# One-core decode kernel: group rows gathered on VectorE, shared weight loads for w2 and wo, w4 in seven pieces

## The chip, the cores and the metric

The kernel runs on one core of one Trainium2 chip. The metric is the device time of one execution in microseconds (us); a few executions are taken for each kernel, in rounds beside the kernel before on the same chip. The profile of one of them gives the trace (the trace of before is of a further execution, outside the timed ones). The *span* that a profile prints runs from the first to the last instruction and is about 1.8 us shorter than the time of the same execution (403.8 and 405.56). All executions here count as undisturbed ("fast") by the usual test.

Engines: PE is the matrix engine, PEld its weight loads, DVE is VectorE, ACT is ScalarE, POOL is GpSimd, SP issues the loads.

## The reference, cut to what matters

Two blocks read the same normalised row and are added. Block A is attention for one token: 32 query heads, 4 key/value heads, 65,536 keys. Block B is a small mixer with two linear layers w1 and w2 and an MLP w3, w4.

```python
x = A_x; xn = _layernorm(x)
out = x + A(xn, k_cache, v_cache, wq, wo) + B(xn, w1, w2, w3, w4)
# A: q = xn @ wq; softmax(q k^T / sqrt(128)) v, then @ wo       (4096 x 1024)
# B: h = gelu(layernorm(xn) @ w1), each quarter of h shifted along the sequence;
#    with a sequence of one, every shifted quarter is zero
#    x1 = xn + hs @ w2;  out = x1 + gelu(layernorm(x1) @ w3) @ w4   (w4: 3584 x 1024)
```

Everything is bf16. The caches are 67 MB each and the weights 36 MB, so 169.87 MB have to be read, once. As the shifted h is zero, w2 multiplies zeros and w1's result is not used; both kernels compute them all the same.

## The kernel before: the parts that matter

All inputs stream through three buffers of 8 MB in a fixed order: wq, w3, w1 and w2 together, then K and V of eight units (K7, wo, V7 at the end), then w4. When a buffer is released, the next load is issued. The result is summed in one bank, `psB`: the left half of the output row in partition 0, the right half in partition 32.

```python
W4_PIECES = (16, 8, 2, 1, 1)        # chunks of 256 KB, one DMA each

def row_acc(j, lhsT, rhs):           # one row of output, half j, on its own column tile
    nc.tensor.matmul(psB[32 * j:32 * j + 1, :], lhsT=lhsT, rhs=rhs, start=False, stop=False,
                     tile_position=(0, 32 * j), skip_group_check=True)

def group_rows(g, og, lp):           # gather the eight heads of a group out of 128 x 512
    for cg in range(4):              # fp32 matmuls against a 0/1 matrix
        nc.tensor.matmul(pe[:, 0:P], lhsT=selbig[:, cg, :], rhs=og[:, 128 * cg:128 * (cg + 1)], ...)
    nc.tensor.matmul(pe[:, P:P + 1], lhsT=sel8big[:], rhs=lp[:, 0:1], ...)
    ...                              # mask, reduce, divide -> oT[g], 128 x 8 bf16

def project(g):                      # oT[g] times its part of wo
    for j in range(8):
        for h2 in range(2):
            row_acc(h2, oT[g][:, j:j + 1], wt[:, g, j, 512 * h2:512 * (h2 + 1)])

compute_k(NU - 1)
for g in range(HKV - 1):
    project(g)                       # groups 0 to 2, while V7 is on its way
compute_v(NU - 1)                    # V7, then group_rows(3)
project(HKV - 1)
compute_w4(0, FC)                    # 28 chunks x 2 matmuls into psB
# copy psB to SBUF, store 2 KB
```

A pass over the finished program drops a weight load when the same weights already stand at the same tile position.

## Time and profile before

The first three timed executions took 404.04 to 404.27 us, median 404.18. The profiled one took 405.56 us.

| what | value | where |
|---|---|---|
| bytes read | 169.87 MB at 421 GB/s | page, queues |
| 16 DMA engines busy with the inputs | 97.6% of the span | page, queues |
| PE busy, DVE busy | 59%, 49% | page, engines |
| wait of PE before the last 24 matmuls | 2.22 us | timeline |

From the profile page of the kernel before, the head, the DMA part and one line of the groups (line of the source, engine, operation, output and inputs, count, then busy us and mean ns, then idle time before and who ended it):

```profile
span 403.8 us, 2690 instructions
...
q1 hardware_dynamic: 4128, 169.87, 97.6%
q8 instruction: 9, 0.15, 0.1%
...
L180 PE MATMUL psB<-big,hT 128*1 128x512 bf16 x56 | 8.1, 452 | 2.2 <-DMA big<-in_B_w_dram 2.2
```

The input queue is nearly always busy. "q8 instruction" is nine packets of 16 KB with which an engine's program itself is fetched.

The PE part of the timeline of the kernel before, from V7 to the end (start us, us, engine, line, operation, then idle time before and who ended it):

```profile
386.08 1.16 PE L398 MATMUL pm_e<-og,selbig 128*128 128x128 f32 x8 [0.86 <-DVE og L389]
387.07 0.28 PE L399 MATMUL pm_e<-lp,sel8big 128*128 128x1 f32 x2
388.41 1.89 PE L180 MATMUL psB<-big,oT 128*1 128x512 bf16 x16 [1.06 <-DVE oT L409]
390.14 3.62 PE L180 MATMUL psB<-big,hT 128*1 128x512 bf16 x32
395.98 4.44 PE L180 MATMUL psB<-big,hT 128*1 128x512 bf16 x24 [2.22 <-DMA big<-in_B_w_dram]
```

Read from below: the last 24 matmuls of w4 take 185 ns each, where the 32 before them took 113 ns. The windows view of the same trace shows why (stretch, its length, busy us and counts of PE, PEld, DVE, ACT and POOL, then the granted clock of PE, the mean share of the DMA engines that is busy, GB/s):

```profile
393.19:396.61 3.42, 1.20 (x12) 0.40 (x10) 0.00 (x0) 0.00 (x0) 0.00 (x0) 1.00 0.69 271
396.60:400.00 3.40, 3.40 (x18) 1.08 (x16) 0.00 (x0) 0.00 (x0) 0.00 (x0) 0.50 0.03 12
```

After a stretch of 3.42 us with the 2.22 us wait in it, the clock is halved for the next 3.41 us. The Trainium skill says in "TensorE: Matmul & The Clock Gate", Part 1, that PE's clock is set by a free-running window of about 3.4 us and halves after an idle one; the clock steps of this trace are indeed multiples of 3.413 us.

One more reading is needed, and the printed views give it only in part: when each load has landed. A load is done when the slowest of the 16 DMA engines is ("DMA: Bandwidth & Descriptors", section "Why a DMA increments its semaphore by 16 and not by 1", says that they finish independently). The trace agrees: for the last chunk of w4 the first engine is done at 395.12 us and the last at 398.42.

### The profile page before, as it was taken

What the parts mean: (1) busy time and instruction counts of PE and PEld (TensorE: products, weight loads), DVE (VectorE), ACT (ScalarE), POOL (GpSimd) and SP (SyncE); (2) the same over time, 40 slices, a digit from 0 to 9 for tenths busy, and PEclk for the clock granted to TensorE, in tenths of its full rate; (3) what the DMA queues carried; (4) which work ended last, traced back from release to release, by engine and by line L of the source; (5) the groups of instructions that cost most, each with busy time, mean ns of one, the idle gap of its engine ahead of it and who ended that gap; (6) DMA issues with size and microseconds to landing.
All of it is one profiled execution on the core that took longest, in us unless ns stands there. A gap on an engine that the chain in (4) does not pass through costs nothing.

```text
span 403.8 us, 2690 instructions
## 1 busy us (share of the span) xinstructions
PE 236.7 (59%) x1392; PEld 51.5 (13%) x952; DVE 197.1 (49%) x141; ACT 27.0 (7%) x35; POOL 5.5 (1%) x29
## 2 busy tenths in 40 slices
PE   5161972691678349742955394649265923787384
PEld 2010110010200120010102110201030101002131
DVE  4000000965296459525943793288439651964010
ACT  1000020003000200020001002000200020002000
POOL 2000000000000000000000000000000000000000
PEclk9995776597679686958896698659776978798698
DMA  9999999999999999999999999999999999999992
GB/s 403 428 392 410 446 454 467 422 416 416 424 461 461 416 411 422 428 474 430 416 422 435 443 441 435 416 428 443 448 435 422 411 435 407 430 476 428 403 409 80
DMA packets 4144, 170.03 MB, mean 421 GB/s; under 512 B 419, under 2 KB 421, under 8 KB 806
## 3 DMA queue, kind: packets, MB, share of 16 engines
q1 hardware_dynamic: 4128, 169.87, 97.6%
q8 instruction: 9, 0.15, 0.1%
q14 instruction: 1, 0.01, 0.0%
q10 hardware_dynamic: 6, 0.00, 0.0%
HBM read 169.87 MB, written 0.00 MB: 421 GB/s over the span
## 4 chain that ended last, share of the span: by engine, by line
DMA 51%; DVE 18%; PE 14%; ACT 2%; issue 0%; SPq 0%; DVEq 0%; ACTq 0%
DMA big<-in_A_k_cache_dram 43%; DVE big L325 14%; DMA big<-in_B_w_dram 8%; PE sc L330 7%; PE oacc L380 4%; PE psB L180 2%; DVE p_sb L351 2%; DVE mx L335 2%; ACT p_sb L348 2%; PE ps L301 1%; PE pm_mx L337 0%; DVE m L339 0%; PE pm_mx L344 0%; DVE rep L341 0%; ACT out_t L438 0%
## 5 line engine op out<-in xcount | busy, mean ns | idle before, releaser
L330 PE MATMUL sc<-big,qdiag 128*128 128x512 bf16 x512 | 129.9, 415 | 62.6 <-DVE big L325 62.4
L325 DVE STREAM_TRANSPOSE big<-big 128x4096 f32<-128x4096 f32 x32 | 139.4, 4413 | 50.6 <-DMA big<-in_A_k_cache_dram 50.6
L380 PE MATMUL oacc<-big,p_sb 128*32 128x512 bf16 x512 | 46.2, 540 | 41.9 <-DVE p_sb L351 34.5
L330 PEld LDWEIGHTS <-qdiag 128*128 128x128 bf16 x128 | 13.2, 103 | 173.0 <-issue 140.7
L335 DVE TENSOR_REDUCE mx<-sc 128x1 f32<-128x2048 f32 x8 | 18.3, 2292 | 29.9 <-PE sc L330 29.9
L348 ACT ACTIVATE p_sb<-sc,nball 128x2048 bf16<-128x2048 f32 x8 | 15.7, 1967 | 219.0 <-DVE nball L346 219.0
L351 DVE STREAM_TRANSPOSE p_sb<-p_sb 128x2048 bf16<-128x2048 bf16 x8 | 18.5, 2311 | 18.0 <-ACT p_sb L348 18.0
L380 PEld LDWEIGHTS <-p_sb 128*32 128x32 bf16 x512 | 17.2, 130 | 68.1 <-DVE p_sb L351 35.1
L247 PE MATMUL psh<-big,ln_rep_b 128*32 128x512 bf16 x56 | 14.2, 1049 | 8.6 <-DMA big<-in_B_w_dram 8.6
L389 DVE SCALAR_TENSOR_TENSOR og<-oacc,wb,og 128x512 f32<-128x512 f32 x4 | 3.0, 750 | 30.7 <-PE oacc L380 30.7
L337 PE MATMUL pm_mx<-ident_f,mx 128*1 128x128 f32 x8 | 2.4, 296 | 19.1 <-DVE mx L335 19.1
L247 PE MATMUL psq<-big,ln_rep_a 128*32 128x512 bf16 x64 | 6.2, 571 | 11.2 <-DMA big<-in_A_wq_dram 11.2
L293 DVE CAST hT<-pm_h 128x24 bf16<-128x24 f32 x1 | 0.3, 264 | 25.1 <-PE pm_h L291 25.1
L180 PE MATMUL psB<-big,oT 128*1 128x512 bf16 x64 | 8.9, 443 | 1.1 <-DVE oT L409 1.1
L259 DVE CAST q_row<-psq 128x512 bf16<-128x512 f32 x1 | 0.7, 691 | 18.1 <-PE psq L247 18.1
L180 PE MATMUL psB<-big,hT 128*1 128x512 bf16 x56 | 8.1, 452 | 2.2 <-DMA big<-in_B_w_dram 2.2
L274 POOL COPY qdiag<-qx 32x32 bf16<-32x32 bf16 x16 | 3.2, 203 | 280.0 <-PE sc L330 250.5
L398 PE MATMUL pm_e<-og,selbig 128*128 128x128 f32 x32 | 4.6, 288 | 3.5 <-DVE og L389 3.5
L344 PE MATMUL pm_mx<-ident_f,rep 1*128 1x1 f32 x8 | 1.8, 228 | 5.0 <-DVE rep L341 5.0
L386 ACT COPY og<-oacc 128x512 f32<-128x512 f32 x4 | 2.3, 586 | 33.7 <-PE oacc L380 33.7
L398 PEld LDWEIGHTS pm_e<-og,selbig 128*128 128x128 f32 x32 | 3.9, 191 | 5.4 <-DVE og L389 5.4
L337 PEld LDWEIGHTS pm_mx<-ident_f,mx 128*1 128x1 f32 x8 | 0.6, 79 | 28.2 <-DVE mx L335 28.2
(96 smaller groups left out, 65.2 us busy)
## 6 DMA issues: line engine op xcount, KB each, us to landing
big<-in_A_wo_dram SPq DMA_DIRECT2D x1, 8192.0 KB, 37.2
big<-in_B_w_dram SPq DMA_DIRECT2D x1, 7168.0 KB, 38.5
big<-in_B_w_dram SPq DMA_DIRECT2D x3, 2048.0 KB, 40.8
big<-in_B_w_dram SPq DMA_DIRECT2D x1, 4096.0 KB, 27.4
big<-in_B_w_dram SPq DMA_DIRECT2D x1, 512.0 KB
big<-in_B_w_dram SPq DMA_DIRECT2D x2, 256.0 KB, 33.3
big<-in_A_k_cache_dram SPq DMA_DIRECT2D x8, 41.7
big<-in_A_v_cache_dram SPq DMA_DIRECT2D x8, 36.8
```

The lines of the kernel that those rows point to most:

```text
L180: nc.tensor.matmul(psB[32 * j:32 * j + 1, :], lhsT=lhsT, rhs=rhs, start=False, stop=False, tile_position=(0, 32 * j), skip_group_check=True)
L247: nc.tensor.matmul(acc[32 * q:32 * q + 32, i, :], lhsT=rep[:, c, :], rhs=cols(c, 2 * q + i), start=(c == 0), stop=(c == DC - 1), tile_posi ...
L274: nc.gpsimd.tensor_copy(out=qdiag[at, LEAD:].rearrange("p (x c) -> p x c", x=4)[:, :, 32 * a:32 * a + 8], in_=qx[at, :, 8 * g:8 * g + 8])
L301: nc.tensor.matmul(ps1[32 * q:32 * q + 32, 0, :], lhsT=xn2_rep[:, c, :], rhs=wt[:, 0, c, 512 * q:512 * (q + 1)], start=(c == 0), stop=(c = ...
L325: nc.vector.transpose(out=words, in_=words)
L330: nc.tensor.matmul(sc[:, e, :], lhsT=qdiag[:, c0:c0 + P], rhs=cols[:, s, e, :, b2, :, r], start=(s == 0 and b2 == 0 and r == 0), stop=(s = ...
L335: nc.vector.reduce_max(out=mx[:], in_=sc[:].rearrange("p e n -> p (e n)"), axis=AX.X)
L337: nc.tensor.transpose(pm[0:1, 0:P], mx[:, 0:1], ident_f[:])
L348: nc.scalar.activation(out=p_sb[:], in_=sc[:], func=ACTF.Exp, bias=nball[:, b:b + 1], scale=SCALE, accum_out=group["lall"][:, b:b + 1])
L351: nc.vector.transpose(out=flat, in_=flat)
L380: nc.tensor.matmul(oacc[32 * q:32 * (q + 1), :], lhsT=pT[:, e, 32 * t:32 * (t + 1)], rhs=vt[:, :, e, t, :], start=(e == 0 and t < 4), stop ...
L398: nc.tensor.matmul(pe[:, 0:P], lhsT=selbig[:, cg, :], rhs=og[:, 128 * cg:128 * (cg + 1)], start=(cg == 0), stop=(cg == 3))
```

## The change

The intent: take the fp32 gather matmuls and many weight loads off PE, and let w4 arrive in pieces that shrink, so that little work is left when the last piece lands. The diff, cut to its core:

```diff
-W4_PIECES = (16, 8, 2, 1, 1)
+W4_PIECES = (11, 6, 4, 3, 2, 1, 1)
...                                   # w1: both halves on one column tile, w2: one zero column for all
-                row_acc(j, gT[:, c:c + 1], wt[:, 1, c, 512 * j:512 * (j + 1)])
+                row_acc(j, g_col[:], wt[:, 1, c, 512 * j:512 * (j + 1)])
...                                   # group_rows
-        for cg in range(4):
-            nc.tensor.matmul(pe[:, 0:P], lhsT=selbig[:, cg, :], rhs=og[:, 128 * cg:128 * (cg + 1)], ...)
-        nc.tensor.matmul(pe[:, P:P + 1], lhsT=sel8big[:], rhs=lp[:, 0:1], start=True, stop=True)
+        nc.vector.tensor_tensor(out=own, in0=own, in1=mask4[:]..., op=ALU.mult)
+        nc.vector.tensor_reduce(out=ol[:, 0:DH], in_=og[:].rearrange("p (s d) -> p d s", d=DH), ...)
+        nc.tensor.matmul(pe[:, 0:DH + 1], lhsT=sel8big[:], rhs=ol[:], start=True, stop=True)
...                                   # project: one column tile, two banks of its own
-                row_acc(h2, oT[g][:, j:j + 1], wt[:, g, j, 512 * h2:512 * (h2 + 1)])
+                nc.tensor.matmul(tail["rows"][0:1, h2, :], lhsT=oT[g][:, j:j + 1], rhs=..., tile_position=(0, 0))
+    def add_projection():
+        rows = ppool.tile([1, 2, 512], F32, name="o_rows", tag="p")
+        nc.vector.tensor_copy(out=rows[:], in_=tail["rows"][0:1, 0:2, :])
+        for j in range(2):
+            row_acc(j, ident_f[0:1, 0:1], rows[0:1, j, :])
...
+    tail["rows"] = ps_S.tile([P, SUBS, 512], F32, name="o_acc", tag="sc")
...
-    compute_w4(0, FC)
+    compute_w4(0, W4_PIECES[0])
+    add_projection()
+    compute_w4(W4_PIECES[0], FC)
```

The two halves of the row now share one weight load in `project`, but they also share one column tile, so they can no longer run side by side (16 matmuls took 1.89 us on two column tiles in before), and their sum has to be added to `psB` at the end.

More of the change, by code (lines that the diff above doesn't have):

```diff
@@ L173, with row_acc @@
     nc.gpsimd.memset(qdiag[:], 0.0)
-    gT = const.tile([P, DC], BF16, name="gT")
-    nc.gpsimd.memset(gT[:], 0.0)
+    g_col = const.tile([P, 1], BF16, name="g_col")
+    nc.gpsimd.memset(g_col[:], 0.0)
     psB = ps_B.tile([P, 512], F32, name="psB")
-    def row_acc(j, lhsT, rhs):
-        nc.tensor.matmul(psB[32 * j:32 * j + 1, :], lhsT=lhsT, rhs=rhs, start=False, stop=False,
+    def row_acc(j, lhsT, rhs, start=False):
+        nc.tensor.matmul(psB[32 * j:32 * j + lhsT.shape[1], :], lhsT=lhsT, rhs=rhs, start=start, stop=False,
                          tile_position=(0, 32 * j), skip_group_check=True)
@@ L223 @@
     nc.vector.tensor_tensor(out=mask16[:], in0=sel32[:, 0:16], in1=sel32[:, 16:32], op=ALU.add)
-    selbig = const.tile([P, 4, P], F32, name="selbig")
-    nc.vector.tensor_copy(out=selbig[:].rearrange("p c (h d) -> p (c h) d", d=16),
-                          in_=sel32[:].unsqueeze(2).to_broadcast([P, 32, 16]))
+    mask4 = const.tile([P, 4], F32, name="mask4")
+    nc.vector.tensor_reduce(out=mask4[:], in_=sel32[:].rearrange("p (s h) -> p s h", h=8), axis=AX.X, op=ALU.add)
     sel8big = const.tile([P, P], F32, name="sel8big")
@@ L239 @@
     for j in range(2):
-        nc.tensor.matmul(psB[32 * j:32 * j + 32, :], lhsT=ident_f[0:1, 0:32], rhs=accx[0:1, 512 * j:512 * (j + 1)],
-                         start=True, stop=False, tile_position=(0, 32 * j), skip_group_check=True)
+        row_acc(j, ident_f[0:1, 0:32], accx[0:1, 512 * j:512 * (j + 1)], start=True)
     def row_matmul(acc, rep, cols, n_slices):
@@ L300, in compute_w12 @@
             for q in range(2):
-                nc.tensor.matmul(ps1[32 * q:32 * q + 32, 0, :], lhsT=xn2_rep[:, c, :],
-                                 rhs=wt[:, 0, c, 512 * q:512 * (q + 1)], start=(c == 0), stop=(c == DC - 1),
-                                 tile_position=(0, 32 * q), skip_group_check=True)
-        h1 = ppool.tile([64, 512], BF16, name="h1", tag="p")
-        nc.scalar.activation(out=h1[:], in_=ps1[0:64, 0, :], func=ACTF.Gelu_apprx_tanh)
+                nc.tensor.matmul(ps1[0:32, q, :], lhsT=xn2_rep[:, c, :], rhs=wt[:, 0, c, 512 * q:512 * (q + 1)],
+                                 start=(c == 0), stop=(c == DC - 1), tile_position=(0, 0))
+        h1 = ppool.tile([32, 2, 512], BF16, name="h1", tag="p")
+        nc.scalar.activation(out=h1[:], in_=ps1[0:32, 0:2, :], func=ACTF.Gelu_apprx_tanh)
         for c in range(DC):
             for j in range(2):
-                row_acc(j, gT[:, c:c + 1], wt[:, 1, c, 512 * j:512 * (j + 1)])
+                row_acc(j, g_col[:], wt[:, 1, c, 512 * j:512 * (j + 1)])
         st.done("w12")
@@ L362, in group_weights @@
         lw = small.tile([P, NB], F32, name="lw")
-        lp = small.tile([P, 1], F32, name="lp")
+        ol = small.tile([P, DH + 1], F32, name="ol")
         nc.vector.tensor_tensor_reduce(out=lw[:], in0=group["lall"][:], in1=wb[:], scale=1.0, scalar=0.0,
-                                       op0=ALU.mult, op1=ALU.add, accum_out=lp[:])
-        return og, wb, lp
+                                       op0=ALU.mult, op1=ALU.add, accum_out=ol[:, DH:DH + 1])
+        return og, wb, ol
     assert NB == 2
@@ L372, in compute_v @@
         if b == 1:
-            og, wb, lp = group_weights()
+            og, wb, ol = group_weights()
         vt = st.tiles[("V", u)][:].rearrange("p (s u t d) -> p s u t d", u=SUBS, s=SETS, t=16)
@@ L390, in compute_v, with group_rows @@
                                        op0=ALU.mult, op1=ALU.add)
-        group_rows(g, og, lp)
+        group_rows(g, og, ol)
     oT = {}
-    def group_rows(g, og, lp):
+    tail = {}
+    def group_rows(g, og, ol):
         pe = ps_M.tile([P, 512], F32, name="pm_e", tag="pm")
-        for cg in range(4):
-            nc.tensor.matmul(pe[:, 0:P], lhsT=selbig[:, cg, :], rhs=og[:, 128 * cg:128 * (cg + 1)], start=(cg == 0), stop=(cg == 3))
-        nc.tensor.matmul(pe[:, P:P + 1], lhsT=sel8big[:], rhs=lp[:, 0:1],
-                         start=True, stop=True)
+        own = og[:].rearrange("p (s d) -> p s d", d=DH)
+        nc.vector.tensor_tensor(out=own, in0=own, in1=mask4[:].unsqueeze(2).to_broadcast([P, 4, DH]), op=ALU.mult)
+        nc.vector.tensor_reduce(out=ol[:, 0:DH], in_=og[:].rearrange("p (s d) -> p d s", d=DH), axis=AX.X, op=ALU.add)
+        nc.tensor.matmul(pe[:, 0:DH + 1], lhsT=sel8big[:], rhs=ol[:], start=True, stop=True)
         msk = small.tile([P, 16, 8], F32, name="msk", tag="msk")
@@ L414, in project @@
             for h2 in range(2):
-                row_acc(h2, oT[g][:, j:j + 1], wt[:, g, j, 512 * h2:512 * (h2 + 1)])
+                nc.tensor.matmul(tail["rows"][0:1, h2, :], lhsT=oT[g][:, j:j + 1],
+                                 rhs=wt[:, g, j, 512 * h2:512 * (h2 + 1)], start=(g == 0 and j == 0),
+                                 stop=(g == HKV - 1 and j == 7), tile_position=(0, 0))
+    def add_projection():
[3 more added lines that the diff above has]
+            row_acc(j, ident_f[0:1, 0:1], rows[0:1, j, :])
     def compute_w4(lo, hi):
```

## The prediction

> **What bounds the kernel now.** The input stream. The page gives 169.87 MB on one queue, with the 16 DMA engines 97.6% busy with it over the 403.8 us span, 421 GB/s; the row of slices is full until the last slice. DMA issues (timeline of SP) come long before they are needed: the next K or V load is issued about 20 us before the previous one has landed, so nothing that PE or DVE does between 40 and 362 us sets the time. Only the tail does. There (timeline, windows of 0.25 us, landings): V7 lands at 380.2, its matmuls end at 385.2, oT is ready at 388.4, projection of group 3 takes 1.9 us, the 16-chunk piece of w4 3.6 us, PE then waits 2.2 us for the 8-chunk piece (395.98), and its last 24 matmuls take 4.4 us, because the granted clock falls from 1.0 to 0.5 at 396.6 after that wait (213 ns a matmul against 113 ns before). The last bytes land at 398.4; matmuls end at 400.4, copy and store end the span at 403.8. So at most about 1.5 us stand between the last landing and the end of PE's work, and that is all the change can win, apart from a small piece of DMA time.
>
> **What the change does, costed.**
> - Body: fp32 gather matmuls of group_rows (8 records, 1.16 us) become two DVE passes of 128x512 fp32 (about 0.7 us each, estimated from the 128x128 and 128x2048 DVE records) and one 129-column matmul. w1 and w2 get fewer loads but w1 loses its two concurrent column tiles. All off the critical path: 0 us.
> - Projection of groups 0 to 2: it now needs the score banks, so it starts after the exp (368.2, not 365.8), and both halves share one column tile, so they no longer overlap: about 216 ns a matmul warm instead of 113. 48 matmuls, the first ten cold, end near 380.5, just as V7 lands. PE is then warm for V7, whose matmuls started cold before (380.3 to 383.0): V7 ends about 0.3 us earlier.
> - Last group: oT at about 388.5, unchanged. Projection of group 3: 16 x 216 ns = 3.5 us, +1.6 us. Then 11 chunks (2.4 us), add_projection (two fp32 512-column matmuls, about 1.5 us warm; the setup ones took 1.9 us each), 17 chunks (3.8 us): PE busy without a gap from 388.5 to about 399.8, so warm. The Trainium skill ("TensorE: Matmul & The Clock Gate", Part 1) has the clock halved after an idle window of about 3.4 us; this trace agrees, its clock steps being multiples of 3.41 us.
> - w4 in seven pieces: more packets, about 0.2 us of engine time, but no 8-chunk lump.
> - PE's instruction count falls by about 110. The trace has nine 16 KB instruction fetches, one per about 256 PE instructions; the last, at 392.1, delayed one DMA engine by about 1.1 us in the tail. With 2257 instead of 2367 instructions it may vanish: last landing near 397.5.
>
> Sum: the tail turns from DMA-late and cold to PE-bound and warm: end of matmuls 400.4 -> about 399.7. Predicted 403.4 us, 8 in 10 between 402.3 and 404.8. Faster by over 2%: 1%; within 2%: 98%; slower: 1%.
>
> **What would show it.** Input queue still about 97.6% busy and at 421 GB/s; no 2.2 us wait of PE before w4's second piece; granted clock 1.0 from 388 to 399; projection of group 3 near 3.5 us; eight instruction fetches, none after 385.
>
> **What would make it wrong.** PE throttled during the 3 us of DVE work before oT: projection and w4 cold, +2 us. Or V7 held up by the serial projection. Or add_projection costlier than 1.5 us. Any of these stays under 1%.

## The result, and the profile after

| | median us | executions |
|---|---|---|
| before | 404.21 | 404.04 to 404.37 (6) |
| after | 404.65 | 403.57 to 405.05 (6) |

The ratio is 1.0006, 95% interval 0.9993 to 1.002: the same. (A ratio is the mean time of one kernel's fast runs over that of the other's of the same rounds, so not quite the ratio of the medians. "The same" means within 2%, and by that rule every run below is the same as before. What is read below are tenths of a percent; the interval leaves out 1 for four runs only: gather alone and old pieces in after, slower, and after with PE kept busy and gap work without w1 and w2, faster.) The median lies inside the predicted range of 402.3 to 404.8, well above its centre of 403.4. The spread is new: 1.5 us, where before had 0.3.

The page of after, the lines that answer to those of before:

```profile
span 402.6 us, 2590 instructions
...
q1 hardware_dynamic: 4416, 169.87, 98.0%
q8 instruction: 9, 0.15, 0.2%
...
L180 PE MATMUL psB<-big,hT 128*1 128x512 bf16 x56 | 7.3, 378 | 0.0
```

The wait for w4 is gone (0.0). The same stretch of PE's timeline in after:

```profile
386.35 0.49 PE L398 MATMUL pm_e<-ol,sel8big 128*128 128x129 f32 x2 [2.63 <-DVE ol L397]
386.76 1.03 PE L180 MATMUL psB<-big,hT 128*1 128x512 bf16 x8
387.90 4.58 PE L413 MATMUL o_acc<-big,oT 128*1 128x512 bf16 x13
...
392.76 1.88 PE L180 MATMUL psB<-big,hT 128*1 128x512 bf16 x12
394.58 1.02 PE L180 MATMUL psB<-o_rows,ident_f 1*1 1x512 f32 x4
...
395.53 3.83 PE L180 MATMUL psB<-big,hT 128*1 128x512 bf16 x34
```

PE is busy without a gap from 387.9 until the output copy at 399.40, and the last chunk of w4 has landed by 397.21. So in this execution PE ends the kernel, 2.2 us after the data. Two things are slow: the projection of the last group, at 350 ns a matmul, and the addition in fp32. The windows view gives the reason for the first:

```profile
384.38:387.79 3.41, 1.44 (x10) 0.56 (x10) 2.72 (x7) 0.00 (x0) 0.00 (x0) 1.00 0.95 404
```

While DVE masks and sums (2.72 us of DVE work in this window), PE does 1.44 us; the trace's clock record has half clock from 387.79 to 391.21.

At first sight the span fell from 403.8 to 402.6 us and the time did not. The answer is in the times of the profiled executions: 405.56 us for before, 1.4 us above the median of its timed ones, and 404.47 for after, a usual one. The trace on which the prediction was built was of an unusual execution. That had to be settled first.

### The profile page after: what moved, and what is told of

The parts are those of the page before. It is cut to its first block, busy times and chain, and to the rows that moved or that the text cites. A ratio compares the mean times of both kernels' runs of the same rounds, so it can differ in the third digit from the quotient of the medians.

```text
span 402.6 us, 2590 instructions
## 1 busy us (share of the span) xinstructions
PE 240.7 (60%) x1364; PEld 46.6 (12%) x870; DVE 204.8 (51%) x150; ACT 27.4 (7%) x35; POOL 5.5 (1%) x29
## 4 chain that ended last, share of the span: by engine, by line
DMA 42%; PE 23%; DVE 18%; ACT 2%; issue 1%; DVEq 0%; ACTq 0%
DMA big<-in_A_k_cache_dram 32%; DVE big L322 11%; DMA big<-in_A_v_cache_dram 10%; PE sc L327 10%; PE oacc L377 7%; DVE p_sb L348 2%; DVE mx L332 2%; ACT p_sb L345 2%; PE psB L180 2%; PE ps L299 1%; PE o_acc L413 1%; DVE ol L397 1%; DVE og L386 0%; DVE og L396 0%; PE pm_e L398 0%
## 5 line engine op out<-in xcount | busy, mean ns | idle before, releaser
L327 PE MATMUL sc<-big,qdiag 128*128 128x512 bf16 x512 | 131.7, 420 | 57.5 <-DVE big L322 51.9
L377 PE MATMUL oacc<-big,p_sb 128*32 128x512 bf16 x512 | 44.2, 521 | 34.7 <-DVE p_sb L348 34.5
L413 PE MATMUL o_acc<-big,oT 128*1 128x512 bf16 x64 | 17.1, 434 | 2.5 <-ACT p_sb L345 2.4
L245 PE MATMUL psq<-big,ln_rep_a 128*32 128x512 bf16 x64 | 5.2, 498 | 11.4 <-DMA big<-in_A_wq_dram 11.4
L398 PE MATMUL pm_e<-ol,sel8big 128*128 128x129 f32 x8 | 2.3, 370 | 10.6 <-DVE ol L397 10.6
L299 PE MATMUL ps<-big,ln_rep_b 128*32 128x512 bf16 x16 | 5.3, 507 | 0.0
L413 PEld LDWEIGHTS <-oT 128*1 128x1 bf16 x32 | 3.0, 93 | 15.5 <-issue 14.8
```

What stands on the lines that cost most here:

```text
L245: nc.tensor.matmul(acc[32 * q:32 * q + 32, i, :], lhsT=rep[:, c, :], rhs=cols(c, 2 * q + i), start=(c == 0), stop=(c == DC - 1), tile_posi ...
L299: nc.tensor.matmul(ps1[0:32, q, :], lhsT=xn2_rep[:, c, :], rhs=wt[:, 0, c, 512 * q:512 * (q + 1)], start=(c == 0), stop=(c == DC - 1), til ...
L327: nc.tensor.matmul(sc[:, e, :], lhsT=qdiag[:, c0:c0 + P], rhs=cols[:, s, e, :, b2, :, r], start=(s == 0 and b2 == 0 and r == 0), stop=(s = ...
L377: nc.tensor.matmul(oacc[32 * q:32 * (q + 1), :], lhsT=pT[:, e, 32 * t:32 * (t + 1)], rhs=vt[:, :, e, t, :], start=(e == 0 and t < 4), stop ...
L413: nc.tensor.matmul(tail["rows"][0:1, h2, :], lhsT=oT[g][:, j:j + 1], rhs=wt[:, g, j, 512 * h2:512 * (h2 + 1)], start=(g == 0 and j == 0), ...
```

## The experiments

Twelve runs were made, two of them of the unchanged kernels. All gave the right output. The main theory: only the tail matters, and its end is the later of two chains, the last landing of w4 and PE's work after V7. Its first rival: the input stream alone sets the time and the differences are noise. A second rival: seven pieces, or fewer loads, change the time by themselves.

### A second trace of before

The kernel is unchanged.

> The kernel before, unchanged, for a second trace: its profiled run took 405.56 us while its timed runs took 404.04 to 404.37, and the profiled run of after took 404.47 with a span of 402.6. Tail theory (the end is set by the last landings plus cold PE work): in a typical run the instruction fetch near 392 us falls on a DMA engine that is not the last one, the last landing comes near 397.3 instead of 398.4, and the span is near 402.4. Rival (the span of 403.8 is typical): span 403.8 again with the last landing near 398.4.

Measured: 403.92 us for the profiled execution, span 402.1; four executions, 403.92 to 405.64. PE's timeline at the end:

```profile
391.70 3.62 PE L180 MATMUL psB<-big,hT 128*1 128x512 bf16 x32
396.00 2.75 PE L180 MATMUL psB<-big,hT 128*1 128x512 bf16 x24 [0.69 <-DMA big<-in_B_w_dram]
```

The span is as the theory said, its reason is not: the last landing is at 398.33, as late as in the first trace. What differs is the clock. In both traces the wait ends when the eight-chunk piece has landed (395.94 and 395.96 us), but in the first one V7's matmuls ended at 385.2 instead of 386.8, so PE got there sooner and waited longer. Here PE waits 0.69 us, stays at full clock, and does the 24 matmuls at 115 ns each; the output is copied at 398.80, not 400.46. (In this trace PE's own run of 24 matmuls and the last landing end together: the last two matmuls start at 398.37.) So before has two modes. In the common one it ends 0.5 us after the last landing; in the rare one PE is caught at half clock, 1.7 us later. Of 55 executions of before, 11 took 405.3 us or more and 44 took 403.8 to 404.4. Each mode was traced once; that the other executions are of the same two kinds is read from their times alone. In its common mode nothing can be won in before by having less PE work at the end. The 1.5 us of the prediction were those of the rare mode.

### Each part alone

Pieces alone is one line:

```diff
-W4_PIECES = (16, 8, 2, 1, 1)
+W4_PIECES = (11, 6, 4, 3, 2, 1, 1)
```

> Before with seven w4 pieces and nothing else. Tail theory: PE no longer waits for an 8-chunk piece and has two to four matmuls left when the last chunk lands; 403.1 us (402.6 to 403.6), about 1.1 us under before. Rival 1 (the input stream alone sets the time, the tail is noise): within 0.2 us of before. Rival 2 (seven pieces cost DMA time): 0.2 to 0.5 us over before.

Measured: 404.09 us (403.96 to 404.27), ratio 0.9998 (0.9985 to 1.001). The expected gain of 1.1 us is not there; for the median the first rival was right. The trace says why, in its last two waits:

```profile
397.27 1.03 PE L180 MATMUL psB<-big,hT 128*1 128x512 bf16 x6 [0.43 <-DMA big<-in_B_w_dram]
398.55 0.38 PE L180 MATMUL psB<-big,hT 128*1 128x512 bf16 x2 [0.25 <-DMA big<-in_B_w_dram]
```

PE now waits for every small piece, two matmuls are left when the last one lands, and that one lands at 398.51. The pieces do what they were made for, but they shorten the chain that wasn't the later one. What they may well remove is the rare mode: no execution of this kernel and of the two below that share its tail, 16 in all, took over 404.5 us. (With a fifth of the executions of before in the rare mode, 16 without one would come by chance in about 3 of 100 cases.)

The projection alone is the `project` and `add_projection` part of the diff above, with the old pieces.

> Before with the projection of wo on shared weight loads into its own banks and added at the end, old pieces. Tail theory: V7 runs warm and ends 1.4 us earlier, the serial projection of group 3 costs 1.6 us more, the addition 1 us; 404.0 us (403.6 to 404.8). Rival 1: within 0.2 us of before. A third reading (fewer weight loads are a gain): over 0.5 us under before.

Measured: 404.08 us (403.96 to 404.32), ratio 0.9998. The result fits the theory and, on the time alone, the rival as well. The parts in the trace: the serial projections of groups 0 to 2 last until V7 has landed, so V7's matmuls run at full clock and end at 384.8, against 386.8 in the second trace of before; the last projection takes 3.6 us, not 1.9; the addition takes 1.02 us. Gain and loss cancel, and the last landing (398.48) covers the rest.

The gather alone is the `group_rows` part of the diff.

> Before with group rows masked and summed on VectorE. Tail theory: oT of the last group comes about 1 us later, while the PE wait for the 8-chunk piece takes up 1 to 2 us of it, but PE is more likely to be throttled after the 3 us without matmuls; 404.4 us (403.9 to 405.4). Rival 1: within 0.2 us of before.

Measured: 405.40 us median, at the upper edge of what was expected; ratio 1.0026 (1.0001 to 1.0051). There are two groups: three executions near 404.3 and three near 406.5. The profiled one is of the slow group:

```profile
388.97 0.80 PE L399 MATMUL pm_e<-ol,sel8big 128*128 128x129 f32 x2 [2.64 <-DVE ol L398]
390.84 3.58 PE L180 MATMUL psB<-big,oT 128*1 128x512 bf16 x16 [1.07 <-DVE oT L408]
394.21 6.88 PE L180 MATMUL psB<-big,hT 128*1 128x512 bf16 x56
```

From the end of V7 to oT it takes 4.4 us here (4.1 in after, 3.1 in before), most of it without PE. The clock is halved from 388.74 to 395.57, the projection takes twice its time, and PE ends 4 us after the data (last landing 397.22, output copy at 401.14). So of the three parts the gather is what harms, and in this execution mostly through the clock. The three executions near 404.3 took about what before takes; their clock was not traced.

### Old pieces in after

```diff
-W4_PIECES = (11, 6, 4, 3, 2, 1, 1)
+W4_PIECES = (16, 8, 2, 1, 1)
```

> After with the five w4 pieces of before (16, 8, 2, 1, 1). In the trace of after, the first eight w4 matmuls run while VectorE gathers the last group, because the 11-chunk piece has landed by 386.6; with a 16-chunk piece that lands near 389.8 they cannot. Tail theory (PE's chain ends after; pieces matter only through these eight matmuls): 0.5 to 1 us over after, near 405.3, and the matmuls end near 400.3. Rival (the pieces do nothing): as after, 404.65. Rival (seven pieces cost): under after.

Measured: 407.35 us (405.61 to 407.59), ratio to before 1.0064 (1.004 to 1.0088). The direction is the theory's, the size is over twice what was expected (0.5 to 1 us over after). In its trace the eight w4 matmuls in the gap are gone, as said, and the clock is then halved for two windows (386.83 to 393.66), not for one. So inside after the seven pieces are worth 2.0 to 2.7 us by the medians (407.35 against 405.39 and 404.65, of other sessions), against nothing in before. The likely reason is that in after PE's chain is the later one, and that the first piece gives PE work just in the gap; the share of each was not separated.

### After with PE kept busy in the gap

```diff
+        if g == HKV - 1:
+            idle = ps_O.tile([P, 512], F32, name="oacc")
+            for i in range(9):
+                nc.tensor.matmul(idle[0:1, :], lhsT=hT[:, 0:1], rhs=st.tiles["wo"][:, 0:512], start=True, stop=True)
         own = og[:].rearrange("p (s d) -> p s d", d=DH)
```

The nine matmuls write a bank that nobody reads; they can start only when DVE has read V7's sums.

> After with nine idle matmuls on PE while VectorE masks and sums the last group. Tail theory (PE throttled after the gap of the gather, which costs the projection and part of w4 in some phases of the clock window): projection of group 3 near 3.5 us in every run, the spread of after (403.57 to 405.05) shrinks to under 0.6 us, the median falls to about 403.5. Rival (the spread comes from the input stream): same spread and median as after.

Measured: 403.57 us (403.34 to 403.72, six executions), ratio to before 0.9979 (0.9964 to 0.9995). Added useless work makes the kernel faster (after itself had 1.0006 and 1.002, in other sessions) and takes the spread away: 0.4 us, where after had 1.5 and 3.2.

```profile
385.00 2.10 PE L398 MATMUL oacc<-big,hT 128*1 128x512 bf16 x9 [0.87 <-DVE og L386]
...
388.59 2.97 PE L417 MATMUL o_acc<-big,oT 128*1 128x512 bf16 x13
```

The projection's 13 matmuls take 2.97 us, not 4.58, and the output copy starts at 398.47. The clock record has full clock from 372.29 to 403.01; the window with the gather in it now holds 3.31 us of PE work:

```profile
385.94:389.36 3.42, 3.31 (x20) 0.81 (x13) 1.75 (x5) 0.00 (x0) 0.00 (x0) 1.00 1.01 426
```

### A second trace of after

The kernel is unchanged.

> After, unchanged, for a second trace and for its spread beside the others on the same chip. Tail theory: again 403.5 to 405.1 us, spread by the phase of the clock window: where this trace's projection of group 3 runs at half clock it takes over 4.5 us and the span is near 403, where it runs at full clock it takes 3.5 us or less and the span is near 401.8. The last landing is 397.2 in either case.

Measured: six executions, 403.10 to 406.25, a wider spread than the expected 403.5 to 405.1; median 405.39; ratio 1.002 (0.9997 to 1.0044). The profiled one has a span of 401.0, the shortest of all traces of before and after (its time, 403.74, is 2.7 us more than the span, where others are 1.8 to 1.9; why was not looked into), and full clock from 371.30 to 402.02:

```profile
384.95:388.36 3.41, 1.88 (x13) 0.72 (x12) 2.27 (x6) 0.00 (x0) 0.00 (x0) 1.00 1.00 422
...
387.93 2.97 PE L413 MATMUL o_acc<-big,oT 128*1 128x512 bf16 x13
...
393.94 3.83 PE L180 MATMUL psB<-big,hT 128*1 128x512 bf16 x34
```

The same program, with the same oT time to 0.1 us, copies its output at 397.81 instead of 399.40. (The first line is the windows view: 1.88 us of PE work in the window of the gather, where the first trace had 1.44.) The difference of 1.6 us is one window of 3.41 us at half clock. By the times, after is up to 1 us faster than before in its fast mode and up to 2 us slower in its slow ones, and the two sessions, with medians of 404.65 and 405.39, drew different shares. (Two executions of the twelve were traced, and none over 404.5 us; what the slowest ones do is not shown.)

### Why the last landing is at 398.4 in some kernels and at 397.2 in others

In the fast mode, after beats the last landing of before by more than 1 us: its data are all there at 397.2. The instruction fetches are the suspect. The landing records of each load show it: in the second trace of before, after the fetch at 43.7 us one engine of 16 finishes about 1.2 us behind the others, after that at 104.2 two do, and with every further fetch there is one more, until by V7 seven engines finish at 378.1 to 378.4 and nine at 379.2 to 380.1 (one of them was set back by an 8 KB packet of another queue). The ninth fetch, where it comes among the last pieces of w4, meets an engine that is late already: fifteen engines finish the last chunk by 397.2, one at 398.33.

Such a delay stands also in the wait of the first trace of before: fifteen engines had finished the eight-chunk piece by 394.80 us, the last one at 395.94, so about 1.1 of the 2.22 us of that wait are a fetch too. And even 397.2 is not free of fetches: in all fourteen traces seven engines finish the last chunk by 395.9 us, and the other nine, the one with the ninth fetch aside, between 396.2 and 397.5; no run removed those fetches, so what they cost the kernel is open.

What does the moment of the ninth depend on?

Sixty tiny matmuls behind the copy of the output, on the pieces kernel:

```diff
+    trash = ps_S.tile([P, SUBS, 512], F32, name="trash", tag="sc")
+    for i in range(60):
+        nc.tensor.matmul(trash[0:1, 0, 0:8], lhsT=out_t[0:64, 0:1], rhs=out_t[0:64, 0:8], start=True, stop=True)
```

> The pieces-only kernel with 60 tiny matmuls behind the copy of the output, which nothing waits for. It asks what the ninth instruction fetch depends on. If on how far PE is from the end of its program (it came with 74 to 81 PE instructions left in five of six traces): it comes after 396.5 and the last landing is near 397.2 instead of 398.5; the matmuls of w4 end near 397.9. If on the count from the start (about 2293): the fetch stays near 393.5 and the last landing near 398.5. The time itself may be prolonged by the 60 matmuls.

Measured: 403.92 us (403.80 to 404.12); ninth fetch at 391.8, after 2285 PE instructions (2293 without the sixty); last landing 398.46. So it isn't the distance to the end of the program. That the fetch comes 1.7 us earlier than in the pieces kernel need not be an effect of the sixty: PE was that much earlier (V7's matmuls end at 385.2, not 386.5), as in the two traces of before, whose fetches are at 392.1 and 393.8.

Fewer PE instructions before the tail, on the pieces kernel (w1 and w2 as in after, the gather of groups 0 to 2 on VectorE, the last one on PE):

```diff
+        if g < HKV - 1:
+            ...                      # group_rows of after
+        else:
+            ...                      # group_rows of before
```

> The pieces-only kernel with about 70 PE instructions fewer before the tail: w1 and w2 as in after, group rows of groups 0 to 2 on VectorE; the last group and all projections as in before. If the fetch depends on the count from the start, it comes about 70 instructions later in PE's work, after the data; last landing 397.2, matmuls end near 397.8, about 403.0 us, 1 us under before: faster than both kernels. If it depends on the distance to the end, nothing changes: last landing 398.5, 404.1 us.

Measured: 404.16 us (403.94 to 404.44); ninth fetch at 394.3, after 2251 PE instructions; last landing 398.83. A miss for the simple count too: the fetch moved by 0.8 us, not behind the data. The rule that fixes the moment stays open.

Then a kernel with a short PE chain. The last projection goes straight into `psB` on two column tiles, and the rows of groups 0 to 2 are added in DVE's gap:

```diff
+        if g == HKV - 1:
+            copy_projection()         # ScalarE, into a buffer that V7 releases
+            add_projection()
+            idle = ps_O.tile([P, 512], F32, name="oacc")
+            for i in range(5):
+                nc.tensor.matmul(idle[0:1, :], lhsT=hT[:, 0:1], rhs=st.tiles["wo"][:, 0:512], start=True, stop=True)
...
+                if g == HKV - 1:
+                    row_acc(h2, oT[g][:, j:j + 1], rhs)
```

> After, but the last group's projection goes straight into the output accumulators on two column tiles, and the rows of groups 0 to 2 are copied by ScalarE and added by PE while VectorE gathers the last group, with five idle matmuls besides. PE's chain should be about 2.5 us shorter than in the idle-matmul kernel (serial projection 1.1, addition 1.0), so that w4 waits for its landings. If the ninth fetch still comes after the data, last landing 397.2, matmuls end 397.7, 402.8 us. If PE being earlier brings the fetch back among the data (near 392 to 395), the last landing is 398.4 again and the time 403.9 us, no better than the idle-matmul kernel (403.57): then PE's lateness is what had kept the fetch out of the way.

Measured: 403.53 us (402.83 to 404.48), ratio to before 0.9985 (0.997 to 1.0001). The fetch stayed at 396.7 and the last landing at 397.29; but in the profiled execution the clock was halved from 389.02 to 392.44 in spite of the work in the gap, 2.35 us in the window before:

```profile
385.61:389.02 3.41, 2.35 (x14) 0.48 (x9) 2.07 (x6) 0.00 (x0) 0.00 (x0) 1.00 0.98 413
```

The spread is back, and this is the likely reason.

The same without the matmuls of w1 and w2, 42 traced PE instructions fewer at 57 us (2229 instead of 2271), the tail untouched (the output stays right, as said above):

```diff
-        ps1 = ps_S.tile([P, SUBS, 512], F32, name="ps1", tag="sc")
-        ...                           # 16 matmuls of w1, gelu, 16 matmuls of w2
         st.done("w12")
```

> The same without the matmuls of w1 and w2, whose result is multiplied by zero or never read, so the output stays right; about 50 PE instructions fewer, 25 us into the kernel, nothing changed in the tail. It asks whether the count of PE instructions before the tail moves the fetch: if so, the fetch comes later than in the gap-work kernel and, if it falls behind 396.6, the time is 402.8 us. If not, as the gap-work kernel.

Measured: 402.76 us (402.68 to 402.91, five executions), ratio to before 0.9966 (0.9954 to 0.9979): faster than both kernels. There is no ninth fetch at all, and in its trace the clock stayed full, though the window of the gather holds the same 2.35 us of PE work:

```profile
span 400.9 us, 2562 instructions
...
q8 instruction: 8, 0.13, 0.1%
...
386.04:389.45 3.41, 2.35 (x14) 0.64 (x11) 1.69 (x5) 0.00 (x0) 0.00 (x0) 1.00 1.02 432
```

And the one that tests the fetch itself. To that kernel, 130 tiny matmuls are added where w1 and w2 stood, in time that PE has to spare; the tail is the same, instruction for instruction:

```diff
+        idle = ps_S.tile([P, SUBS, 512], F32, name="idle", tag="sc")
+        for i in range(130):
+            nc.tensor.matmul(idle[0:32, 0, 0:8], lhsT=xn2_rep[:, 0, :], rhs=wt[:, 0, 0, 0:8], start=True, stop=True)
         st.done("w12")
```

> The gap-work kernel without w1 and w2 matmuls, plus 130 tiny matmuls (8 columns) where those stood, near 57 us, when PE has time; the tail is the same, instruction for instruction. It asks whether the ninth instruction fetch itself makes the last landing late. If it does: nine fetches instead of eight, the ninth among the data between 385 and 395, the last landing 398.3 to 398.8 instead of 397.27, and about 403.9 us instead of 402.76. If the late landing has another cause in the tail of the kernels that showed it: last landing 397.3 and 402.8 us, whatever the fetch does.

Measured: 404.10 us (403.72 to 404.23, another chip; ratio to before 0.9982, 0.996 to 1.0003, in a session where five of eleven executions of before were of the rare mode); nine fetches, the ninth at 392.69; last landing 398.6. The last wait of PE in the kernel without them and in this one:

```profile
397.31 0.38 PE L180 MATMUL psB<-big,hT 128*1 128x512 bf16 x2 [0.26 <-DMA big<-in_B_w_dram]
```

```profile
398.66 0.38 PE L180 MATMUL psB<-big,hT 128*1 128x512 bf16 x2 [0.21 <-DMA big<-in_B_w_dram]
```

Both waits are for data. And the windows of the kernel with nine fetches show what is still moving after 397 us:

```profile
397.00:397.50 0.50, 0.50 (x8) 0.25 (x6) 0.00 (x0) 0.00 (x0) 0.00 (x0) 1.00 0.06 25
397.50:398.00 0.50, 0.50 (x8) 0.19 (x5) 0.00 (x0) 0.00 (x0) 0.00 (x0) 1.00 0.06 25
```

A share of 0.06 is one engine of 16, at 25 GB/s, with all others done. In the kernel with eight fetches the same stretch has a share of 0.00. The 130 matmuls take 3.4 us at 57 us, and with them comes a ninth fetch of 16 KB and a last landing that is 1.3 us later: this is shown. The time is less clean. As the output copy started 0.46 us after the last landing in both, the late landing is enough to explain the 1.3 us. But this trace also had half clock from 389.30 to 392.71, which the trace without the 130 had not, and PE came to its last two matmuls late on its own account: its pairs of matmuls start every 0.215 us up to 398.08, so the last pair, at 398.66, waited only about 0.37 us longer than PE's own pace. With the data there earlier, this execution would have ended about 0.4 us sooner, not 1.3. For the price of a fetch in time the better evidence is across kernels: the five traces below with full clock at the end and a last landing of 398.3 to 398.8 copy their output 0.46 to 0.47 us after it, just as the one without a ninth fetch does after 397.27.

All traces together, in the order of the ninth fetch. The columns come from the packet and landing records of the traces and from the start of the output copy in their timelines:

| kernel | ninth fetch us | last landing us | output copy us | span us |
|---|---|---|---|---|
| pieces and 60 trailing | 391.8 | 398.46 | 398.93 | 402.1 |
| before, first trace | 392.1 | 398.42 | 400.46 | 403.8 |
| gap work, no w1 and w2, 130 more | 392.7 | 398.6 | 399.08 | 402.3 |
| projection alone | 393.3 | 398.48 | 398.94 | 402.3 |
| pieces alone | 393.5 | 398.51 | 398.97 | 402.2 |
| before, second trace | 393.8 | 398.33 | 398.80 | 402.1 |
| pieces, fewer instructions | 394.3 | 398.83 | 399.29 | 402.5 |
| gather alone | 396.7 | 397.22 | 401.14 | 404.5 |
| after, first trace | 396.7 | 397.21 | 399.40 | 402.6 |
| after, PE kept busy | 396.7 | 397.29 | 398.47 | 401.7 |
| gap work | 396.7 | 397.29 | 398.45 | 401.7 |
| after, old pieces | 399.4 | 397.02 | 402.07 | 405.4 |
| after, second trace | after the span | 397.27 | 397.81 | 401.0 |
| gap work, no w1 and w2 | none | 397.27 | 397.73 | 400.9 |

Seven traces with the fetch by 394.3 have a last landing of 398.3 to 398.8; seven with a later one or none have 397.0 to 397.3.

## Why the prediction was right or wrong

The time lies in the range and "the same" was right. Point by point:

- *"The input stream ... Only the tail does."* Right as far as tested. No experiment that changed the body (fewer instructions at 57 us, gathers of groups 0 to 2) moved the time except through the tail.
- *"at most about 1.5 us stand between the last landing and the end of PE's work, and that is all the change can win."* This is the step that failed. The 1.5 us (2.0 from landing to copy) belong to an execution of 405.56 us. In the common mode, read from the second trace, the copy starts 0.5 us after the landing, so a shorter PE chain wins next to nothing: pieces alone, 404.09. Nor is the wait before the last 24 matmuls only a matter of the eight-chunk lump, as the prediction has it: about half of it was the fetch. The 405.56 beside the median of 404.18 should have been taken for a warning.
- *"PE busy without a gap from 388.5 to about 399.8, so warm."* Wrong in the trace of after and, by the times, in most of its executions; right in its second trace. PE was busy, but the clock is decided by the window before, in which DVE gathers. It was named under what would make the prediction wrong, at 2 us; it measured 1.6.
- *"oT at about 388.5, unchanged."* 387.9, but as a sum of two errors: V7 ends 1.5 to 3.0 us earlier, not 0.3 (383.7 against 385.2 and 386.8 in the two traces of before), and the gather takes 1 us more. Its reduction took 1.02 us, not 0.7.
- *"Projection of group 3: 16 x 216 ns = 3.5 us, +1.6 us."* Right at full clock: 3.6 us with two w4 matmuls mixed in, in the second trace. *Add_projection 1.5 us*: 1.02.
- *"With 2257 instead of 2367 instructions it may vanish: last landing near 397.5."* Right in effect: 397.21, but not as a fetch that vanished. The sign asked for, eight fetches and none after 385, failed: there are nine, the ninth at 396.7, after the data. This is the one true gain of the change, 1.1 us, and the change wasn't made for it. Whether fewer PE instructions or a later PE moved the fetch is not separated; the gather alone moved it as far (396.7), seventy instructions fewer did not (394.3).
- In sum, fast mode against fast mode: V7 3.0 us earlier, gather 1.0 later, PE's time after oT 1.0 longer (serial halves and addition, less the w4 matmuls done in the gap and less the 0.7 us that before spends waiting): copy at 397.81 against 398.80. The slow modes of after give that back and more. The centre of 403.4 us was a subtraction from the wrong trace. That the median came within 1.3 us of it, and inside the range, was luck: the gain was taken from a mode that is rare, and the losses by the clock, named as a risk, were left out of the sum.

## What to carry to other kernels

Before building on a profile, compare the time of the profiled execution with the median of the timed ones; if it differs, it shows a mode, and a second trace is cheap. Where a kernel ends on a stream of loads, find which chain is the later one at the end, last landing or compute, before shortening either, and look at what else uses the DMA engines in the last few microseconds: here one 16 KB instruction fetch among the last loads made the last landing 1.1 to 1.3 us later. When work goes from PE to another engine near the end, count what the gap does to PE's clock; here nine matmuls that compute nothing made the kernel faster.

## What the Trainium skill lacked or had wrong

- "Runtime: NRT & Kernel Launch", section "Instruction fetch mechanics", says that programs are refilled in 16 KiB blocks of 256 instructions and that crossing a block is "mostly hidden". The traces agree on the size (nine packets of 16 KB for about 2,400 PE instructions). They show a cost that the section doesn't name, hidden or not from the engine that runs the program: the fetch shares the DMA engines with the inputs and delays one of them by about 1.1 us. 130 added matmuls that cause one more fetch among the last loads moved the last landing from 397.27 to 398.6 us (and the time from 402.76 to 404.10, where a halved clock played a part too).
- "TensorE: Matmul & The Clock Gate", Part 1, speaks of an idle window. Here half clock followed windows of 3.41 us in which PE was busy for 1.20 us (before) and 1.44 us (after), while 1.88 us kept the clock in the second trace of after. No single share of busy time separates them: 2.35 us were followed by half clock in the gap-work kernel and by full clock in the one without w1 and w2. What counts as busy stays open.
- The same page, in its closing table, advises against PE-idle gaps over about 3 us. In the first trace of before a wait of 2.22 us was enough.
- No page tells at which instruction of a block the next fetch is issued. Kernels with 2256 or more traced PE instructions had nine fetches, the one with 2229 had eight. The ninth came after 2210 to 2293 of them, tied neither to the distance from the end (60 trailing matmuls left it at 2285) nor simply to the count from the start: in the two traces of after, the same program, it came after 2210, at 396.7 us, and after all 2256, behind the span.
